# A Mamba-2 scan joined to a low-rank mixer on one core: state updates, copies of y and joins as pieces of their own, and a new order after piece w5

## The chip, the core and the metric

The kernel runs on one core of one Trainium2 chip. The metric is the device time of the execution in microseconds (us). The kernel before was run three times: 225.86 us is the median, 225.63 the lowest and 227.96 the highest. The profile is of one execution, whose span from the first to the last instruction is 224.7 us.

## What is computed

The first stage is a chunked state-space scan over x (4 batches, 8 heads, 768 positions, 32 channels), with decays a and projections B and C of 16 states. Its result, laid out as batch x 768 x 256, goes through a mixer: a low-rank product over the positions (U, V of rank 32), and a two-layer network over the channels (256 to 1024 to 256).

```python
# scan, per chunk of the sequence
L = np.exp(cum[:, :, :, None] - cum[:, :, None, :]) * causal
y_intra = np.einsum('bhij,bhjd->bhid', CB * L, xc)
y_inter = np.einsum('bhin,bhnd->bhid', Cc, state) * decay_to_i[:, :, :, None]
state = decay_full[:, :, None, None] * state + np.sum(Bx, axis=2)
...
# mixer
h = x.transpose(0, 2, 1) @ U @ V
u = x + h.transpose(0, 2, 1)
ch = np.maximum(u @ w_ch1, 0.0) @ w_ch2
return (u + ch).astype(np.float32)
```

## The kernel before, in words

The whole kernel is one list of pieces written out by hand: the string PLAN (line 36). Each word is a letter, which names a kind of piece, and numbers, which say for which block it is done. The function follow (line 859) reads the words from left to right and emits each piece's instructions, and every engine runs its own instructions in exactly that order. An engine whose next instruction waits holds up all that stand behind it. So the order of the words is the order of work on TensorE (PE), VectorE (DVE), ScalarE (ACT), GpSimd (POOL) and SyncE (SP, whose queue issues all DMAs).

The scan works on 12 blocks k of 256 positions, three for each batch (k = 3b + q). Its pieces:

- b, x, B, X, L: DMA loads of B, C and x; w, W, Z, z: loads of the mixer's weights, which come as 64-bit words. The pieces B, X, w and L wait, before their first DMA is issued, for the last DVE instruction that was emitted ahead of them (the list until, line 864).
- P (prep, one DVE product), T (turned: four transposes by PE in two halves, and after the second half three ACT copies; bank w), g (gram: 32 small matmuls into two x and two z banks), m and M (mask: two DVE operations each; m reads the x banks and M the z banks), s (state: small matmuls into two w banks), u (update: up to four chained DVE operations of 128x64, then one POOL product), i and j (inter: small matmuls with the state; j is preceded by the POOL copy "settled", line 576, which waits for the products of the same bank pair that stand before it), n (intra: 64 small matmuls), y (yout: two ACT copies out of the two y banks), t (transposes by PE, and a copy).

The mixer runs per batch b:

- c (to_fp32, line 398): the four steps in which DVE and ACT turn a weight's 64-bit words into fp32; R (refine): the steps that split a weight into near, far and joined parts for the batches 1 to 3.
- p, q, a: the low-rank product; S (split): one ACT and two DVE operations of 128x768 that split u into three parts, for a half j of the sequence.
- For batch 0: U (plain: fp32 matmuls with a relu by ACT) and d0 (down with fp32 matmuls).
- For batches 1 to 3, in a faster number format: f (first: four matmuls of 384 columns into a bank x or z, then an ACT scaling), e (second: two matmuls more into that bank, then an ACT relu), h (third: one DVE operation of 128x384 that makes the far part and lets the bank go, and for every odd m a further one, joined, line 710, of 128x768 that makes the joined part of both m of a pair), d (down: six pieces n = 0 to 5 of four matmuls of 256 columns for each output block k; the last adds one matmul, a DVE addition and the output DMA). Pieces 0 and 1 of d read the near parts, 2 and 3 the far parts, 4 and 5 the joined parts.

PSUM has eight banks, two under each of the names w, x, z and y. A piece that needs a bank waits until the piece that had it two allocations ago has been read out. In SBUF, 15 buffers called words are shared by the weights' words, their conversion and the parts that f, e, h and d use.

Of the kernel before, what the change touches and what calls it, by code (L numbers as in the profile page):

```python
# [76 lines left out]
def kernel(  # L77
# [64 lines left out]
    def bank(tag, *dims):  # L142
        t = psum.tile([P, *dims], FP32, tag=tag, name=tag, bufs=BANKS[tag])
        return t
# [75 lines left out]
    w1all = mix.tile([P, NQ, NCB, W], FP32, tag="u", name="w1f", bufs=1)  # L220
    w1f = [w1all[:, c] for c in range(NQ)]
    w2 = [const.tile([P, NM, DM], FP32R, name=f"w2{i}") for i in range(2)]
    weights = []
    w2f, w2b = {}, {}

    def w2c(n, dtype):
# [25 lines left out]
    def load_v():  # L252
        own["UV"] = words_of(UV)
        for q in range(4):
            begin(out=own["UV"][ts(q, Q), 2 * NC * RK:], in_=V2[:, ts(q, 2 * NC * RK)])
# [653 lines left out]
```

## Time and profile before

| what | value |
|---|---|
| median of 3 runs | 225.86 us (225.63 to 227.96) |
| span of the profiled execution | 224.7 us |
| first instruction of the new order (U0.0.0 on PE) | 34.84 us |
| last row of matmuls in the chain ends | 221.15 us |
| PE, DVE, ACT, POOL busy | 96%, 70%, 51%, 6% |
| granted TensorE clock | 1.00 throughout |

The profiled execution's own time isn't listed apart from the three runs; its span is 1.16 us below their median, which is the work around the first and the last instruction.

How to read it: a busy PE isn't PE at its peak, since matmuls overlap and their ends are modelled. Start to start of the pieces tells more, and the chain of waits gives that: each row of it is a time, how long the chain stayed there, the engine, the tile written, the line and how many instructions. In this kernel a row of 16 matmuls on line 613 is an i or j, of about 53 on line 635 an n, of 4 on line 656 a t, of 2 on line 480 half of T, about 32 on line 543 an s, rows on line 511 a g, and on line 725 x4 with tiles x or z a U or an f.

### The profile page before, as it was taken

The page shows a single profiled execution, that of the slowest core. Times are in us where ns is not written, and L with a number is a line of the kernel's source. Part 1 is how long each engine was busy: PE and PEld are TensorE (multiplying, and loading weights), DVE is VectorE, ACT ScalarE, POOL GpSimd, SP SyncE. Part 2 cuts the span into 40 slices and gives each one's busy share as a digit, 9 for nine tenths or more (in the row PEclk, how much of TensorE's full clock was granted, in tenths as well). Part 3 has the DMA queues.
Part 4 walks back from the last instruction along what each step waited for, and adds up shares of the span by engine and source line. Part 5 has one row for each costly group of instructions (what it writes and reads, how often), then busy time and mean ns, then how long its engine had stood idle before and what let it go on. Part 6 is the DMA issues. An engine that isn't in the chain of part 4 may idle for free.

```text
span 224.7 us, 7010 instructions
## 1 busy us (share of the span) xinstructions
PE 216.0 (96%) x3012; PEld 182.8 (81%) x3012; DVE 156.7 (70%) x329; ACT 114.3 (51%) x261; POOL 14.3 (6%) x37
## 2 busy tenths in 40 slices
PE   7888989999999999999999999999999999999993
PEld 4656655656668898987999898887998999999993
DVE  4776878899998866969717785758437964764921
ACT  3334946856994346334453632475237545655410
POOL 3021010012100000202101000100000000000000
PEclk9999999999999999999999999999999999999999
DMA  6997799788645203600002602000020000100011
GB/s 88 127 111 144 132 130 287 139 163 230 92 65 72 51 23 59 84 23 26 3 26 48 96 0 73 3 3 3 1 71 1 0 0 26 47 0 28 32 38 47
DMA packets 69518, 14.56 MB, mean 65 GB/s; under 512 B 63792, under 2 KB 67696, under 8 KB 69488
## 3 DMA queue, kind: packets, MB, share of 16 engines
q1 hardware_dynamic: 69488, 14.13, 34.6%
q8 instruction: 23, 0.38, 0.7%
q14 instruction: 7, 0.06, 0.1%
HBM read 10.98 MB, written 3.15 MB: 63 GB/s over the span
## 4 chain that ended last, share of the span: by engine, by line
PE 91%; DVE 2%; DMA 2%; SPq 1%; issue 1%; POOL 0%; ACT 0%; POOLq 0%; DVEq 0%
PE x L725 31%; PE z L725 24%; PE y L725 12%; PE y L613 4%; PE y L635 3%; PE w L480 3%; PE x L511 3%; PE w L656 2%; DMA bc<-in_B_dram 2%; PE w L543 2%; PE z L511 2%; PE x L138 1%; SPq L185 1%; PE w L679 1%; PE w L138 1%
## 5 line engine op out<-in xcount | busy, mean ns | idle before, releaser
L159 DVE SCALAR_TENSOR_TENSOR words<-words 128x768 fp32r<-128x768 f32 (+6 forms) x44 | 34.6, 806 | 1.9 <-ACT words L416 0.6
L725 PE MATMUL z<-u,w 128*128 128x384 f32 x144 | 34.0, 350 | 0.0
L725 PE MATMUL x<-u,w 128*128 128x384 f32 x144 | 33.1, 348 | 0.0
L730 ACT ACTIVATE x<-x 128x384 f32<-128x384 f32 (+1 forms) x30 | 13.6, 452 | 25.3 <-PE x L725 25.1
L725 PEld LDWEIGHTS z<-u,w 128*128 128x128 f32 x144 | 24.5, 188 | 1.3 <-DVE words L159 0.2
L725 PEld LDWEIGHTS x<-u,w 128*128 128x128 f32 x144 | 24.0, 188 | 1.3 <-ACT x L730 0.6
L159 DVE SCALAR_TENSOR_TENSOR words<-x,words 128x384 fp32r<-128x384 f32 x24 | 13.2, 555 | 16.4 <-ACT words L759 13.7
L725 PE MATMUL x<-w2c,words 128*128 128x256 f32 x112 | 22.5, 338 | 0.0
L730 ACT ACTIVATE z<-z 128x384 f32<-128x384 f32 (+1 forms) x27 | 12.5, 463 | 14.1 <-PE z L725 13.6
L725 PEld LDWEIGHTS x<-w2c,words 128*128 128x128 f32 x112 | 18.2, 189 | 1.3
L725 PE MATMUL y<-w,words 128*128 128x256 f32 x144 | 19.1, 282 | 0.0
L725 PEld LDWEIGHTS y<-w,words 128*128 128x128 f32 x144 | 18.5, 188 | 0.3 <-DVE ytok L159 0.3
L159 DVE SCALAR_TENSOR_TENSOR words<-z,words 128x384 fp32r<-128x384 f32 x24 | 13.2, 551 | 5.7 <-ACT words L759 5.7
L759 ACT ACTIVATE words<-x 128x384 fp32r<-128x384 f32 x24 | 11.6, 490 | 6.3 <-PE x L725 6.1
L759 ACT ACTIVATE words<-z 128x384 fp32r<-128x384 f32 x24 | 11.6, 491 | 4.9 <-PE z L725 4.8
L648 ACT COPY yT<-y 128x256 f32<-128x256 f32 x24 | 7.8, 384 | 10.9 <-PE y L613 10.7
L569 POOL TENSOR_TENSOR Sm<-S,own 128x256 f32<-128x256 f32 (+1 forms) x12 | 7.7, 644 | 87.5 <-DVE S L159 58.1
L159 DVE SCALAR_TENSOR_TENSOR S<-S,kept,w 128x64 f32<-128x64 f32 x40 | 11.2, 280 | 2.7 <-PE w L543 0.9
L613 PE MATMUL y<-T,Sm 32*64 32x64 f32 x352 | 12.4, 239 | 0.4 <-POOL Sm L569 0.3
L725 PE MATMUL x<-w,words 128*128 128x256 f32 x96 | 12.6, 282 | 0.0
L725 PEld LDWEIGHTS x<-w,words 128*128 128x128 f32 x96 | 12.0, 188 | 0.1
L511 PE MATMUL x<-Cm,T 32*64 32x128 f32 x192 | 11.0, 307 | 1.0 <-ACT Cm L490 0.7
(152 smaller groups left out, 400.5 us busy)
## 6 DMA issues: line engine op xcount, KB each, us to landing
words<-in_moe_w_ch_dram SPq DMA_DIRECT2D x7, 512.0 KB, 6.1
x<-in_x_dram SPq DMA_DIRECT2D x24, 128.0 KB, 3.7
out_dram<-ytok SPq DMA_DIRECT2D x24, 128.0 KB, 1.7
bc<-in_B_dram SPq DMA_DIRECT2D x24, 64.0 KB, 3.7
bc<-in_C_dram SPq DMA_DIRECT2D x12, 128.0 KB, 3.8
words<-in_moe_w_ch_dram SPq DMA_DIRECT2D x2, 256.0 KB, 4.5
words<-in_moe_V_dram SPq DMA_DIRECT2D x4, 48.0 KB, 3.1
words<-in_moe_U_dram SPq DMA_DIRECT2D x1, 192.0 KB, 3.5
```

The lines of the kernel that those rows point to most:

```text
L138: nc.tensor.matmul(out=t[:, :m * w].rearrange("p (m i) -> p m i", i=w), lhsT=ident, rhs=ident[:, None, :w].to_broadcast([P, m, w]), start= ...
L159: self.last = call(*args, **kwargs)
L480: nc.tensor.transpose(out=tp[:, i, v], in_=s["BC"][:, i, c + v].rearrange("p h n -> p (h n)"), identity=ident)
L511: nc.tensor.matmul(out=g[r][cols, c], lhsT=s["T"][rows, 0, c, cols], rhs=s["Cm"][rows, :, :, ts(2 * c + p, Q)].rearrange("r v t i -> r v i ...
L543: nc.tensor.matmul(out=s["A"][p][ts(r, Q), v], lhsT=s["BC"][half, 0, v, 2 * r:2 * r + 2].rearrange("p h n -> p (h n)"), rhs=x_sb[k][half, ...
L569: nc.gpsimd.tensor_tensor(out=s["Sm"][:, sl], in0=s["S"][:, sl].rearrange("p i (s d) -> p i s d", s=2), in1=own2[:, b, 4 * q + sl.start:4 ...
L613: product = nc.tensor.matmul(out=y[p][ts(r % 2, H), r // 2, c], lhsT=own[ts(r, Q)], rhs=s["T"][ts(r, Q), 1, :, ts(2 * c + p, Q)].rearrange ...
L635: product = nc.tensor.matmul(out=y[p][ts(i, Q), n, c], lhsT=x_sb[k][half, c, h], rhs=s["M"][half, h // 2, c, h % 2], start=fresh(k, p, [i] ...
L648: nc.scalar.copy(out=yp[:, :, :, p], in_=st[k]["y"][p])
L725: nc.tensor.matmul(out=t, lhsT=lhsT, rhs=rhs, start=start, stop=True, skip_group_check=True)
L730: nc.scalar.activation(t, t, AF.Copy, scale=1.0 + EPS)
L759: nc.scalar.activation(gs[j, m // 2][0][:, m % 2], t, AF.Relu, scale=NEAR)
```

## The change

The words u and y become two words each (u4.0 u4.1: the first two and the last two updates of the state; y4.0 y4.1: the copy of one y bank each). The POOL product of u is left as it was: one instruction after the second half. The joined operation leaves h and becomes a piece J with its own place. Up to piece w5 the words and loads stand as they were, with u and y only written as two words; from there on all words are in another order, loads among them. The loaded weights are kept in a dictionary instead of a list, since w8 is now loaded ahead of w7. The number of instructions of each kind stays as it was.

```diff
-    ... 'W2 W3 b5.1 W4 a0.0 c2 c2 a0.1 x4.0 w5 c3 c3 c3 c3 '
-    'U0.0.0 P5 U0.0.1 U0.1.1 R0 B6 t3 X5 g4 m4 T5 M4 T5 c5 c5 U0.1.0 c5 c5 X6 U0.1.3 c4 c4 s4 u4 w6 '
-    'w7 w8 U0.0.3 P6 U0.0.2 c6 U0.0.6 s5 c4 c4 U0.1.7 c6 U0.1.2 u5 R0 R2 U0.1.6 n4 s6 L7 i4 g5 c6 '
-    'j4 y4 u6 T6 T6 m5 c6 R4 R2 R1 U0.0.4 M5 U0.1.4 n5 i5 L8 g6 c7 c7 c9 c9 t4 j5 P7 T7 T7 M6 c7 c7 '
-    'y5 U0.0.7 c8 U0.0.5 t5 m6 n6 R3 c9 c9 P8 c8 p1 R7 g7 m7 L9 i6 M7 T8 T8 c8 c8 q1 d0.0.2.0 '
...
-    'd1.1.0.5 d1.1.2.4 d1.1.2.5 d1.1.1.4 d1.1.1.5 T10 g9 m9 T10 T11 T11 M9 i9 n9 g10 m10 M10 j9 y9 '
-    's11 u11 i10 g11 m11 M11 n10 f2.0.4 a2.1 f2.0.3 f2.0.2 e2.0.4 h2.0.4 e2.0.3 e2.0.2 f2.0.7 '
...
+    'W2 W3 b5.1 W4 a0.0 c2 c2 a0.1 x4.0 w5 U0.0.0 c3 X5 P5 c3 t3 U0.0.1 U0.1.1 c3 T5 T5 w6 c3 g4 m4 '
+    'M4 c4 s4 X6 u4.0 B6 u4.1 U0.0.2 c4 c5 R0 U0.1.0 c4 c5 c5 c5 s5 c6 w8 U0.1.3 U0.0.3 U0.1.2 u5.0 '
+    'u5.1 U0.0.6 P6 c4 n4 c7 s6 u6.0 i4 g5 c6 j4 u6.1 L7 R2 M5 y4.1 y4.0 c7 R1 T6 m5 w7 T6 U0.0.7 '
+    'U0.1.6 c6 n5 i5 g6 c9 c6 j5 c9 R0 y5.0 t4 P7 T7 M6 y5.1 T7 U0.1.5 m6 t5 U0.0.5 R3 n6 c9 c7 i6 '
+    'g7 c8 j6 R1 m7 p1 U0.0.4 M7 c9 q1 U0.1.4 c8 d0.0.1.0 R3 c7 s7 L9 c8 c8 U0.1.7 d0.0.1.1 R2 R4 '
+    'a1.0 S1.0 d0.0.0.0 d0.0.1.2 d0.0.1.3 L8 R6 y6.1 d0.0.0.1 d0.0.0.2 P9 R7 d0.0.0.3 y6.0 f1.0.0 '
+    'f1.0.3 d0.0.2.0 u7.0 d0.0.2.1 P8 u7.1 e1.0.0 d0.0.2.2 d0.0.2.3 e1.0.3 f1.0.5 f1.0.2 h1.0.3 '
+    'h1.0.0 T8 R6 f1.0.7 e1.0.2 d0.1.0.0 e1.0.5 R4 e1.0.7 h1.0.5 d0.1.0.1 d0.1.0.2 h1.0.2 f1.0.1 '
+    'h1.0.7 L10 T8 a1.1 R5 R7 d0.1.0.3 e1.0.1 f1.0.6 d0.1.1.0 f1.0.4 d0.1.1.1 h1.0.1 e1.0.6 d0.1.1.2 '
+    'R5 e1.0.4 h1.0.4 d0.1.1.3 h1.0.6 s8 n7 i7 g8 u8.0 P10 m8 j7 S1.1 T10 y7.1 d0.1.2.0 d0.1.2.1 T10 '
+    'M8 y7.0 f1.1.0 J1.0.3 d0.1.2.2 d0.1.2.3 f1.1.1 f1.1.3 e1.1.0 e1.1.1 J1.0.2 u8.1 s9 n8 u9.0 i8 '
+    'u9.1 h1.1.1 t7 d1.0.2.0 d1.0.2.1 d1.0.2.2 R4 L11 R6 j8 h1.1.0 s10 y8.0 d1.0.2.3 e1.1.3 d1.0.1.0 '
...
+    't8 f1.1.5 J1.1.0 e1.1.2 h1.1.2 f1.1.4 t6 e1.1.5 f1.1.6 e1.1.4 p2 T9 J1.1.1 h1.1.4 h1.1.5 e1.1.6 '
+    'h1.1.6 q2 T9 d1.1.2.0 d1.1.2.1 d1.1.2.2 d1.1.2.3 a2.0 J1.1.2 d1.1.1.0 J1.1.3 S2.0 d1.1.1.1 '
+    'd1.1.2.4 d1.1.1.2 d1.1.1.3 d1.1.0.0 d1.1.0.1 d1.1.0.2 d1.1.0.3 d1.1.1.4 P11 d1.1.2.5 d1.1.0.4 '
+    'd1.1.0.5 d1.1.1.5 s11 u11.0 g9 T11 m9 i9 M9 T11 g10 n9 M10 m10 j9 y9.1 g11 y9.0 n10 i10 M11 m11 '
+    'f2.0.4 a2.1 f2.0.1 e2.0.4 f2.0.6 f2.0.3 h2.0.4 e2.0.1 e2.0.6 j10 e2.0.3 u11.1 f2.0.0 y10.1 '
...
@@ def update(k, c=0, n=2):
-        sl = slice(own[0], own[-1] + 1)
+        if c + n < 2:
+            return
+        sl = slice(0, own[-1] + 1)
...
-    def yout(k):
+    def yout(k, p):
...
-        for p in range(2):
-            nc.scalar.copy(out=yp[:, :, :, p], in_=st[k]["y"][p])
+        nc.scalar.copy(out=yp[:, :, :, p], in_=st[k]["y"][p])
@@ def third(j, m):
-            if m % 2:
-                joined(near, far, both)
+
+        def fourth(j, n):
+
+            joined(*gs[j, n])
...
-                 M=lambda k: mask(k, (2, 3)), u=update, i=lambda k: inter(k, 0), n=intra,
+                 M=lambda k: mask(k, (2, 3)), u=lambda k, c: update(k, c, 1), i=lambda k: inter(k, 0), n=intra,
```

More of the change, by code (lines that the diff above doesn't have):

```diff
@@ L142, in bank @@
     def bank(tag, *dims):
-        t = psum.tile([P, *dims], FP32, tag=tag, name=tag, bufs=BANKS[tag])
-        return t
+        return psum.tile([P, *dims], FP32, tag=tag, name=tag, bufs=BANKS[tag])
     ctx.enter_context(tc.manual_schedule())
@@ L222 @@
     w2 = [const.tile([P, NM, DM], FP32R, name=f"w2{i}") for i in range(2)]
-    weights = []
+    weights = {}
     w2f, w2b = {}, {}
@@ L233, in words_of @@
         t = raw.tile([P, 2 * WCOLS], INT32, tag="words", name="words", bufs=NWORDS)
-        weights.append((dst, t[:p, :2 * i * j]))
         return t[:p, :2 * i * j]
@@ L238, in each, with load_words @@
         return [part[index] for part in parts]
-    def load_words(dst, src):
+    def load_words(n, dst, src):
         p, i, j = dst.shape
         t = words_of(dst)
+        weights[n] = dst, t
         begin(out=t.rearrange("p (i j) -> p i j", i=i), in_=src)
@@ L253, in load_v @@
         own["UV"] = words_of(UV)
+        weights[1] = UV, own["UV"]
         for q in range(4):
@@ L262, in load_w @@
         if n < 2:
-            if n == 0:
+            if "w" not in own:
                 own["w"] = words_of(w1f[0])
-                weights.pop()
             dst, t = w1f[0][:, :, ts(n, P)], own["w"][:, ts(n, 2 * NCB * P)]
-            weights.append((dst, t))
+            weights[2 * n] = dst, t
             begin(out=t.rearrange("p (i j) -> p i j", i=NCB),
@@ L270, in load_w @@
         elif n <= NQ:
-            load_words(w1f[n - 1], w13[:, :, ts(n - 1, 2 * quarter)])
+            load_words(n + 1, w1f[n - 1], w13[:, :, ts(n - 1, 2 * quarter)])
         else:
             m = 2 * (n - NQ - 1)
-            load_words(w2c(n - NQ - 1, FP32), w22[m * P:(m + 2) * P].rearrange(
+            load_words(n + 1, w2c(n - NQ - 1, FP32), w22[m * P:(m + 2) * P].rearrange(
                 "(m p) d -> p m d", p=P))
@@ L567, in update @@
             st["Sm", b, j + 1] = s["Sm"][:, i].rearrange("p s d -> p (s d)")
-        sl = slice(own[0], own[-1] + 1)
+        if c + n < 2:
+            return
+        sl = slice(0, own[-1] + 1)
         nc.gpsimd.tensor_tensor(
             out=s["Sm"][:, sl], in0=s["S"][:, sl].rearrange("p i (s d) -> p i s d", s=2),
-            in1=own2[:, b, 4 * q + sl.start:4 * q + sl.stop, :, None].to_broadcast(
-                [P, len(own), 2, D]), op=ALU.mult)
+            in1=own2[:, b, 4 * q:4 * q + sl.stop, :, None].to_broadcast(
+                [P, sl.stop, 2, D]), op=ALU.mult)
     def apart(k):
@@ L639, in intra @@
                         behind.setdefault(k, []).append(product)
-    def yout(k):
+    def yout(k, p):
         b, q = pairs[k]
-        if q == 0 and b:
+        if b not in yT:
             yT[b] = mix.tile([P, NCB, S], FP32, tag="yT", name="yT")
@@ L796, in mixer @@
         us, gs, gT = {}, {}, {}
-        return SimpleNamespace(p=project, q=parted, a=added, S=split, f=first, e=second, h=third,
+        return SimpleNamespace(p=project, q=parted, a=added, S=split, f=first, e=second, h=third, J=fourth,
                                d=down, U=plain)
```

52 rows, old and new, of the table PLAN are left out of this document.

## Prediction

> **What bounds the kernel now.** I read the page first: the busy shares, the slices and the chain's shares.
>
> ```profile
> span 224.7 us, 7010 instructions
> PE 216.0 (96%) x3012; PEld 182.8 (81%) x3012; DVE 156.7 (70%) x329; ACT 114.3 (51%) x261; POOL 14.3 (6%) x37
> ...
> PE   7888989999999999999999999999999999999993
> ...
> DVE  4776878899998866969717785758437964764921
> ...
> PE 91%; DVE 2%; DMA 2%; SPq 1%; issue 1%; POOL 0%; ACT 0%; POOLq 0%; DVEq 0%
> ```
>
> PE is in nine tenths of the chain and without a visible gap from the seventh slice on. DVE is full only in slices 8 to 13. Next the table by stages, cut where the work changes: the order that stays; the U pieces with batches 1 and 2 of the scan; the d0; then the rest.
>
> ```profile
> 0.00:34.84 34.84, 30.08 (x738) 20.32 (x738) 23.61 (x76) 17.29 (x48) 5.56 (x21) 1.00 0.92 128
> 34.84:68.10 33.26, 33.00 (x587) 20.94 (x588) 31.52 (x71) 26.20 (x56) 3.35 (x5) 1.00 0.74 154
> 68.10:101.60 33.50, 33.50 (x223) 29.76 (x221) 25.30 (x46) 14.48 (x30) 1.47 (x2) 1.00 0.32 52
> 101.60:147.10 45.50, 45.43 (x849) 41.35 (x846) 30.39 (x65) 19.59 (x46) 3.75 (x8) 1.00 0.16 34
> 147.10:221.00 73.90, 73.89 (x627) 70.45 (x625) 45.49 (x73) 36.70 (x83) 0.18 (x1) 1.00 0.06 19
> ```
>
> The columns are the stage's length, then PE, PEld, DVE, ACT and POOL, then the granted clock, which is 1.00 throughout. The first 34.84 us, where PE has its real gaps (4.8 us), belong to pieces whose order stays: nothing is won there. In the second stage DVE is busy 31.52 of 33.26 us, so there PE and DVE are both nearly full. Behind that only PE is.
>
> A busy PE can still be slow, so I go to the chain's rows for what one piece costs at its best and what it costs elsewhere.
>
> ```profile
> 41.48 1.29 PE x L725 x4
> ...
> 44.06 0.38 PE w L543 x32
> 44.45 1.49 PE z L725 x4
> ...
> 151.68 0.70 PE z L725 x4
> ...
> 152.81 0.58 PE w L656 x4
> 153.39 0.35 PE x L725 x2
> 153.75 0.89 PE z L725 x4
> 154.63 0.43 PE y L613 x16
> ```
>
> A U takes 1.29 us after its like and 1.49 behind the small s; an f takes 0.70 among its like and 0.89 between an e that followed a t and an i. So each block of small scan pieces that stands between the large matmuls costs PE about 0.2 us over its own time, without any engine being late. In the old list behind w5 I count 19 such blocks: some 19 x 0.2 = 3.8 us that no better overlap removes, only fewer blocks.
>
> **The change part by part.** No instruction is added or removed. The joined operation (J), the second half of u and the copies of y only move; so PE's own work stays, and the sum has three terms: the number of blocks, the waits that go, the waits that come.
>
> *Blocks.* In the new list I count 24 blocks of small pieces behind w5. The U stretch has 8 in place of 7 that stand up to s7, and the stretch behind it 16 in place of 12: T8 stands alone twice, T10 is parted once, T9 follows q2 alone, t6 stands alone. 5 more blocks at 0.2 us are 1.0 us at most. Blocks that are one T or t may cost less: there is no row for a lone T. The lower end is 0 (a wait of PE that falls into the block hides the switch), the upper 1.0. I take 0.8, near the upper end, since both rows above (1.49 against 1.29, 0.89 against 0.70) have the whole 0.2. The Trainium skill, page "TensorE: Matmul & The Clock Gate", section "Step-by-step: what each phase is for", says that PE pulls the next weight load ahead of running matmuls when the row groups don't conflict or the background weights are free, so that a load overlaps the matmul before it. By that a change of piece would be free and the sum 0.8 us lower; inside a stretch of one kind the trace agrees (four matmuls in 0.70), at the change it doesn't (0.89), so I go by the rows.
>
> *The first scan block behind w5.*
>
> ```profile
> 39.72 0.28 PE x L511 x2
> ...
> 40.85 0.63 PE w L480 x4
> ...
> 40.02 0.68 DVE L159 TENSOR_TENSOR BC<-bc,F 128x512 f32<-128x512 f32 x1
> 40.72 0.76 DVE L159 TENSOR_TENSOR M<-x,causal 128x256 int32<-128x256 int32 x2
> 41.40 0.75 DVE L159 TENSOR_TENSOR M<-z,causal 128x256 int32<-128x256 int32 x2
> ...
> 41.52 0.58 ACT L484 COPY T<-w 128x512 f32<-128x512 f32 x1 [0.66 <-PE w L480]
> 42.00 0.84 ACT L490 ACTIVATE Cm<-w,slot 128x256 f32<-128x256 f32 x2
> ```
>
> Before, g4 runs from 39.72 to 40.85, 1.13 us (g8 took 0.58, rows below): some 0.5 us of wait, for the z bank of U0.1.1, while T5 had its input from P5 at 40.70. In the new list P5 is three DVE operations earlier, so T5 comes straight behind U0.1.1 and g4 behind it: it still waits about 0.25 for the relu of U0.1.1. But s4 now follows g4 at once. It needs both w banks, and T5's bank is let go by the three ACT copies (0.58 and 0.84, ended 1.36 us after T5 itself, 41.48 to 42.84). Of that only g4, with its wait about 0.85, lies over it, and ACT first has the relu of U0.1.1 to do: s4 waits 0.5 to 0.85, I take 0.65, as the relu and T5 end within a half microsecond of each other. 0.9 in place of 0.5: +0.4.
>
> *The scan of batch 3.*
>
> ```profile
> 102.06 0.13 PE x L511
> ...
> 102.64 0.25 PE w L543 x8
> ...
> 137.56 0.28 PE x L511 x2
> ...
> 138.64 0.81 PE w L480 x6
> 139.45 0.42 PE y L613 x12
> ...
> 141.38 0.27 PE y L613 x10
> ...
> 143.69 0.79 PE y L635 x52
> ...
> L648 ACT COPY yT<-y 128x256 f32<-128x256 f32 x24 | 7.8, 384 | 10.9 <-PE y L613 10.7
> L576 POOL COPY settled<-slot 128x1 f32<-128x1 f32 x12 | 4.2, 348 | 46.2 <-PE y L635 32.3 <-PE y L613 14.0
> ```
>
> g8 shows what a g costs, 102.06 to 102.64. Before, g9 took 137.56 to 138.64, so 0.5 of wait (for a z bank that d1.1.1.5's addition frees); j9, s11, i10 and g11 took 141.38 to 143.69, 2.31 us for work of 0.43 + 0.38 + 0.43 + 0.58 = 1.82 (an i or j by the row of i9, an s as at 44.06): 0.5. Together 1.0. In the new list s11 stands ahead of g9 and covers 0.25 of its wait (0.25 left). But g10 comes already after T11, i9 and T11: a cover of 0.22 + 0.43 + 0.22 = 0.87 us (half of T is a third of the row of six, less the switch), while all four banks have to pass m9 and M9, 0.76 + 0.75 on DVE: g10 waits 0.65 to 0.75. j9 follows n9 directly, so "settled" (0.35 on POOL by its mean, behind n9's end) can't start before: 0.35. n10 comes after g11 alone (0.58), with two copies of y9 at 0.38 in front: 0.2. M10 and m10 are covered by n9 and j9. Sum 0.25 + 0.7 + 0.35 + 0.2 = 1.5 in place of 1.0: +0.5.
>
> *The waits that go.* Behind 147.1 the old order takes 73.9 us; the 143 pieces at their best (f 0.69, e 0.35, d 0.47 and 0.59 for the last, the small ones as in the rows) come to 71.4, and its five blocks to 1.0. About 1.1 to 1.5 us of waits are left there, and some 0.3 for s9 and n7 near 103. They stand where an f waits for a bank that h lets go:
>
> ```profile
> L159 DVE SCALAR_TENSOR_TENSOR words<-words 128x768 fp32r<-128x768 f32 x24 | 23.1, 963 | 1.2
> L159 DVE SCALAR_TENSOR_TENSOR words<-x,words 128x384 fp32r<-128x384 f32 x24 | 13.2, 555 | 16.4 <-ACT words L759 13.7 <-PE x L725 1.4 <-ACT z L730 1.2
> ```
>
> Before, each odd h (0.55) drags its joined operation (0.96) behind it, and the next h or addition, which frees a bank, stands behind both on DVE. With J a piece of its own, joins stand behind several h, and their readers d.4 and d.5 come late: J2.0.1 stands twelve pieces ahead of d2.0.1.4, say. Also the e with which PE went straight into a d of the same pair (e2.1.7, d2.1.2.0, d2.1.2.1) now have several pieces between. All of it is 1.4 (1.1 + 0.3), so the gain lies between 0 and 1.4, or below nothing if joins come too late for d.4; I take 0.9, since the DVE isn't full there (45.49 of 73.90), so that an h moved ahead does run ahead. If DVE were full, J would only be late in h's place.
>
> *Loads.* They go through SP in the new order, and hold up nothing on PE by themselves:
>
> ```profile
> words<-in_moe_w_ch_dram SPq DMA_DIRECT2D x7, 512.0 KB, 6.1
> bc<-in_B_dram SPq DMA_DIRECT2D x24, 64.0 KB, 3.7
> ...
> 53.34 0.37 SPq L185 DMA_DIRECT2D bc<-in_B_dram  x1
> ...
> 55.09 2.15 SPq L185 DMA_DIRECT2D x<-in_x_dram  x2
> ```
>
> w8 waits for c6's first step and needs 6.1 us; DVE has ahead of c9's first step two u (8 x 0.28), P6, a step of c4, c7's first, m5 and M5 (1.5) and two operations of c6, some 7 us. Before, L7's five issues took 53.34 to 57.24, 3.9 us; P7's last part is the third of them and lands about 1.6 + 3.7 us after the first issue, and DVE has some 5.4 us of work ahead of P7. w7 stands behind L7 in the queue. All are in time by half a microsecond to one. I count 0 for them, and up to 2 us in the range.
>
> The tail (the last d, its addition and its DMA) stays: 0.
>
> Sum against the profiled execution: 224.7 + 0.8 + 0.4 + 0.5 - 0.9 = 225.5. Its span is 1.16 us below the median of the runs shown, 225.86; I carry that over: **226.7 us**, 0.4% more than before. A measurement of this kernel tells about 1% (2.3 us) from no change: the forecast is no change.
>
> **The rivals.**
>
> *Faster: blocks cost nothing and the waits go.* If the switches hide behind other things (0) and the new order has none of the waits that I place at s4 and g10 (DVE or ACT ahead of my count), it gains all that can be gained: 0.5 + 1.0 + 1.4 = 2.9, so 223.0. For it: the fuller separation of h and J. Against it: s4's two banks and g10's four have a fixed chain of copies or masks in front, with rows for each. It is over 1% only if nearly all goes. The Trainium skill, page "Perfetto Trace Analysis", section "Identifying the Most-Contended Engine", says matmul busy time is no measure of the room on PE, and to take the weight loads' share, here 81%; a reading by it would leave more room than 2.9 us. In the stage behind 147.1, where the weight loads are busy 70.45 of 73.90, the trace says there is little.
>
> *Slower: the loads come late and DVE stands.* Place: c9, c8 and P7 on DVE between 55 and 65 us, where DVE is busy 31.52 of 33.26. If w8, L7 or w7 lands later than 0.5 to 1 us past my count, DVE stands, and everything behind it in its queue: m6, M6 for n6, q1, a1.0, S1.0, f1.0.0. DVE has some slack there: its operations from w5 to S1.0, by the rows, end near 75 us, and the pieces of PE put f1.0.0 at about 78; for n6 and T7 there is less. It decides from 2 us late on; with 4 us late for the three (6.1 us become 10), PE loses about 2.5 us: 229.2. For it: the chain already has 2% of DMA, and six queue rows lie close together. Against: the second stage's DMA share is 0.74 now and nothing is added.
>
> *No effect:* J, u and y move but waits only change places, all terms within 0.3 of zero: 225.9. It is inside the forecast's case.
>
> **How the numbers follow.** Forecast within 1% (223.6 to 228.1): 0.66, the no-effect case included. Faster: 0.10, since it asks for three terms at their ends at once. Slower by over 1%: 0.24, by late loads, or because the s4, g10 and block terms are at their upper ends with no gain behind 147 (1.0 + 0.65 + 0.6, that is 228.1). Range: from 224.4 (blocks 0, gain 1.4) to 229.2 (late loads). It leaves out about 2 in 10.
>
> **What would show each step right or wrong.** Blocks: rows of U at 1.49 and f at 0.89 more often than before, and the stage from w5 to the first d1 longer with no wait named. s4: a gap between g4 and s4 of over 0.4 us, with ACT's Cm copies ended just before s4. Batch 3: g10 over 1.1 us long, and a gap between n9 and j9. J: f and e rows near 150 us without the extra 0.1, and the stage behind it below 73.9 us. Loads: DVE idle before words or BC released by a DMA between 50 and 66 us. Wrong is the prediction if PE shows a wait of over 1 us in a place not named here, or if the blocks turn out free.

## The result

| | kernel before | changed kernel |
|---|---|---|
| median of 18 runs each | 225.93 us | 228.19 us |
| ratio, with its 95% interval | | 1.0088 (1.0061 to 1.0116) |
| span of the profiled execution | 224.7 us | 226.1 us |

The changed kernel is 0.9% slower, which is inside the 1% that the prediction called no change, and inside its range (224.4 to 229.2). The interval leaves out 1, so it is a small slowdown and not noise, about twice the 0.4% that was forecast. The predicted 226.7 us is 1.5 us too low. The median of before rests on more runs here than in the prediction and hardly moved. Executions over 1.5% above the fastest of their kernel are left out of the ratios, "at full clock" below means a granted clock of 0.995 or more over the execution, and a star in a table marks a stretch in which the clock was below 1.00 for a while.

The page of the changed kernel, the lines that answer to those shown of before:

```profile
span 226.1 us, 7017 instructions
...
PE 214.4 (95%) x3012; PEld 181.6 (80%) x3012; DVE 154.6 (68%) x329; ACT 114.5 (51%) x261; POOL 13.2 (6%) x37
...
PE 72%; SPq 8%; DVE 7%; DMA 6%; issue 3%; ACT 1%; POOL 1%; DVEq 0%; POOLq 0%; ACTq 0%
```

PE's work is nearly the same (214.4 us, before 216.0), but PE has 72% of the chain instead of 91%, and the queue, the DMAs and DVE have 21% instead of 5%. That isn't time lost on PE: of the some 42 us by which PE's part of the chain is shorter, 16 us lie ahead of 35.5 us, where the order is unchanged and the chain only follows the DMA queue back from a load. What PE lost is read from the stages. Next the stages, cut at U0.0.0, U0.0.4, s8, f2.0.4 and the last d piece. The columns are again the length, PE, PEld, DVE, ACT, POOL, the clock and the DMA share.

```profile
0.00:35.52 35.52, 29.81 (x739) 19.54 (x739) 23.53 (x76) 17.42 (x48) 5.63 (x21) 1.00 0.91 115
35.52:67.40 31.88, 30.19 (x588) 19.15 (x588) 29.62 (x69) 23.86 (x50) 3.29 (x6) 1.00 0.70 156
67.40:100.62 33.22, 32.77 (x191) 28.03 (x187) 20.18 (x40) 18.42 (x39) 0.62 (x1) 1.00 0.46 65
100.62:147.29 46.67, 46.03 (x860) 41.40 (x860) 34.79 (x71) 17.14 (x41) 2.81 (x6) 1.00 0.16 36
147.29:222.12 74.83, 74.83 (x636) 72.95 (x636) 45.91 (x77) 37.62 (x85) 0.88 (x3) 1.00 0.05 19
```

In the second stage PE now has gaps of 1.69 us (31.88 less 30.19), where before it had 0.26. The last stage is shorter; the same cut of the kernel before is this:

```profile
144.41:220.38 75.97, 75.96 (x641) 72.50 (x636) 47.07 (x78) 37.65 (x85) 0.37 (x2) 1.00 0.06 19
```

75.97 has become 74.83. Stages with other pieces in them can't be subtracted so. For these I take the time from the start of one PE piece to the start of the next, less a fixed time for each kind of piece, what it takes undisturbed among its like (U 1.29 us, f 0.69, e 0.35, d 0.47, n 0.79, half of T 0.22, and so on), and call the sum over a stage its room. Single pieces can come out shorter or longer by 0.2 us, since a start moves when the next piece is of another kind, so the room is used to compare, not as a wait of its own. Behind f2.0.4 and between s8 and the last scan cluster the room of one order comes out the same within 0.1 us in every execution, so one execution is enough there. Room in us, by stages:

| run | first U to last U | f1.0.0 to s8 | s8 to scan of batch 3 | scan of batch 3 | f2.0.4 to end |
|---|---|---|---|---|---|
| before | 2.29 | 0.53 | 1.52 | 1.31 | 2.40 |
| changed | 3.90 | 0.87 | 1.06 | 2.08 | 1.25 |
| a1, changed again | 5.88* | 1.11 | 1.06 | 2.08 | 1.24 |
| e1, b5.1 early | 5.20 | 1.03 | 1.06 | 2.09 | 1.31 |
| e2, L8 ahead of L9 | 5.19* | 1.87 | 1.08 | 2.08 | 1.31 |
| e3, old scan of batch 3 | 5.20 | 0.85 | 1.06 | 1.68 | 1.33 |
| e4, g4 first | 7.04* | 0.95 | 1.06 | 2.08 | 1.25 |
| e5, L9 L8 early | 4.08* | 0.15 | 1.07 | 2.08 | 1.31 |
| e6, T in pairs | 3.77 | 1.53 | 1.59 | 2.24 | 1.25 |
| e7, before with late J | 2.31 | 0.54 | 7.65* | 1.31 | 7.98 |
| e8, b5.1 and x4.0 early | 3.99 | 1.17 | 1.09 | 2.08 | 1.31 |
| e9, old head, new tail | 2.56 | 0.54 | 1.50 | 1.31 | 1.34 |
| e10, before with J spread | 2.19 | 0.53 | 1.51 | 1.31 | 3.54 |
| e11, three mended | 4.68 | 0.15 | 1.07 | 1.68 | 1.33 |

So the loss is in the U stage (+1.6 us here, up to +2.9) and in the scan of batch 3 (+0.77), a late load adds 0.7 us behind f1.0.0, and the last stage gives 1.15 back.

Where the U stage loses, the chain of waits of the changed kernel shows:

```profile
33.60 6.22 DMA bc<-in_C_dram
...
39.94 0.70 DVE BC L161
...
40.78 0.64 PE w L482 x4
...
41.93 0.85 ACT Cm L492 x2
...
42.83 0.43 PE w L545 x24
...
54.27 0.29 DVE S L161
...
54.70 0.63 PE w L482 x4
...
59.49 0.56 POOL settled L580
```

The C of block 5, issued at 33.60, lands 6.22 us later; P5 (39.94) and T5 (40.78) stand for it. s4 (42.83) stands for the copies of T5. T6 (54.70) stands for the second half of u6, now a piece behind j4, and j5, which now follows g6 at once, for "settled" (59.49). And behind f1.0.0:

```profile
81.64 3.55 DMA bc<-in_B_dram
...
85.31 0.69 DVE BC L161
...
86.90 0.97 PE x L728 x4
87.87 0.22 PE w L482 x2
88.09 0.70 PE z L728 x4
```

L8 is issued behind the addition and the output DMA of d0.0.1.3, its last B lands at 85.19, and P8 holds DVE until then; f1.0.2 (86.90) has to wait for an addition behind P8.

### The profile page after: what moved, and what is told of

Its sections match the earlier page's. It is cut to its first block, busy times and chain, and to the rows that moved or that the text cites. A ratio compares the mean times of both kernels' runs of the same rounds, so it can differ in the third digit from the quotient of the medians.

```text
span 226.1 us, 7017 instructions
## 1 busy us (share of the span) xinstructions
PE 214.4 (95%) x3012; PEld 181.6 (80%) x3012; DVE 154.6 (68%) x329; ACT 114.5 (51%) x261; POOL 13.2 (6%) x37
## 3 DMA queue, kind: packets, MB, share of 16 engines
q1 hardware_dynamic: 69488, 14.13, 35.5%
## 4 chain that ended last, share of the span: by engine, by line
PE 72%; SPq 8%; DVE 7%; DMA 6%; issue 3%; ACT 1%; POOL 1%; DVEq 0%; POOLq 0%; ACTq 0%
PE x L728 26%; PE z L728 19%; PE y L728 12%; SPq L187 8%; DMA bc<-in_C_dram 5%; PE y L639 3%; PE y L617 3%; PE w L482 2%; PE w L659 2%; DMA bc<-in_B_dram 2%; DVE words L161 2%; PE x L513 1%; PE w L545 1%; PE z L513 1%; PE w L682 1%
## 5 line engine op out<-in xcount | busy, mean ns | idle before, releaser
L728 PE MATMUL z<-u,w 128*128 128x384 f32 x144 | 32.2, 342 | 0.0
L728 PEld LDWEIGHTS x<-u,w 128*128 128x128 f32 x144 | 24.5, 188 | 1.4 <-DVE ytok L161 0.8
L728 PE MATMUL y<-w,words 128*128 128x256 f32 x144 | 19.6, 281 | 0.0
L651 ACT COPY yT<-y 128x256 f32<-128x256 f32 x24 | 8.4, 376 | 14.0 <-PE y L617 14.0
L161 DVE TENSOR_TENSOR BC<-bc,F 128x512 f32<-128x512 f32 (+2 forms) x18 | 8.9, 510 | 9.5 <-DMA bc<-in_B_dram 6.6
L728 PE MATMUL x<-w,words 128*128 128x256 f32 x96 | 13.6, 285 | 0.0
L617 PE MATMUL y<-T,Sm 32*64 32x64 f32 x352 | 11.9, 240 | 1.1 <-POOL settled L580 0.6
L728 PE MATMUL z<-w2c,words 128*128 128x256 f32 x56 | 12.0, 340 | 0.0
```

The lines of the kernel that those rows point to most:

```text
L161: self.last = call(*args, **kwargs)
L617: product = nc.tensor.matmul(out=y[p][ts(r % 2, H), r // 2, c], lhsT=own[ts(r, Q)], rhs=s["T"][ts(r, Q), 1, :, ts(2 * c + p, Q)].rearrange ...
L651: nc.scalar.copy(out=yp[:, :, :, p], in_=st[k]["y"][p])
L728: nc.tensor.matmul(out=t, lhsT=lhsT, rhs=rhs, start=start, stop=True, skip_group_check=True)
```

## The experiments

### a1: the changed kernel once more

> The changed kernel once more, beside the kernel before on the same chip. Theory A (the loss is late data for VectorE at two places plus a longer tail of the scan of batch 3; the 0.67 us by which U0.0.0 starts later in the changed trace is a matter of one execution, since nothing ahead of it differs): the ratio is again near 1.009, and in the new profile U0.0.0 starts at 34.8 to 35.0 us. Rival B (the start is really later by 0.67 us, through the loads): U0.0.0 starts again at 35.4 us or later.

Measured: 1.0044 (0.9996 to 1.0092), lower than the 1.009 that was expected, with an interval that holds both 1 and 1.0088. U0.0.0 started at 35.98 us here. With a clock of 1.00 ahead of it, it started at 33.96 to 35.98 us in eight executions with this order behind it and at 34.30 to 34.92 in three with the order of before. So its place is a matter of the execution, as theory A has it; the 35.98 alone would have pointed to B.

### e1: one late load moved forward

```diff
- b5.2 b5.0 T4 T4 j3 y3.0 y3.1 W2 W3 b5.1 W4
+ b5.2 b5.0 b5.1 T4 T4 j3 y3.0 y3.1 W2 W3 W4
```

> The changed kernel with one load moved: the C of block 5 (b5.1) is issued right behind the two other loads of block 5 instead of behind W2 W3. In the changed trace P5 on VectorE waits 1.29 us for it, and T5 with its four matmuls stands 0.85 us late. Theory A (this load is what makes the first U pieces dearer): P5 waits less than 0.2 us, the pieces from U0.0.0 to U0.1.4 take 0.9 to 1.4 us less, the time is 0.4 to 0.6 per cent below that of the changed kernel (about 227.0). Rival (the 1.3 us are in VectorE only, and another wait, that of j4 or g6, takes the place): the time is that of the changed kernel, 228.2.

Measured: 1.0031 (0.9988 to 1.0074), no faster than a1 beside it (at full clock the median is 227.62 us for both); the room of the U stage 5.20. P5 no longer waits, but the chain now has another load:

```profile
33.12 8.69 DMA x<-in_x_dram
...
41.94 0.65 PE w L545 x29
```

s4 stands 2.1 us for the first x of block 4, the last load of the same group. DVE, too, has other stands now: 0.71 us for the weights W2, 0.44 for a step of ACT and 1.13 at P6 for the B of block 6. The rival holds: other waits take the place.

### e2 and e5: the loads of block 8 earlier

```diff
 e2
- R3 c7 s7 L9 c8 c8 ... d0.0.1.3 L8 R6
+ R3 c7 s7 L8 L9 c8 c8 ... d0.0.1.3 R6
 e5
+ R3 c7 s7 L9 L8 c8 c8 ... d0.0.1.3 R6
```

> The changed kernel with the loads of block 8 issued ahead of those of block 9, no longer behind the additions of the first d pieces. In the changed trace VectorE stands 3.95 us at P8 for its B. Theory A (late load, 0.6 to 0.7 us of it reach TensorE at f1.0.5 and f1.0.2): the stand of VectorE goes, the time is about 227.5. Rival (TensorE has enough queued, the 0.6 us come from the order of d and f in that stage): the stand of VectorE goes and the time stays within 0.2 us of 228.2.

Measured: 1.0091 (1.0048 to 1.0133), at full clock 228.65 us against a1's 227.62. The rows of P9 and P8 on DVE (in brackets the idle time before, and what ended it):

```profile
84.05 0.69 DVE L161 TENSOR_TENSOR BC<-bc,F 128x512 f32<-128x512 f32 x1 [1.94 <-DMA bc<-in_B_dram]
85.49 0.69 DVE L161 TENSOR_TENSOR BC<-bc,F 128x512 f32<-128x512 f32 x1
```

P9 stands ahead of P8 in the list, and L9 was now second in the queue: the stand moved from P8 to P9, and PE lost 1.62 us at f1.0.3. Neither theory had that. With L9 first:

> The changed kernel with the loads of block 8 issued right behind those of block 9, both ahead of the additions of d. Issuing L8 ahead of L9 moved the stand of VectorE from P8 to P9, since P9 comes first in the order, and TensorE lost 1.6 us at f1.0.3. Theory A (a load that is late for VectorE's next step holds the additions behind it, and so the banks of the f pieces): now neither P9 nor P8 waits over 0.5 us, the room over the shortest times between f1.0.0 and s8 is 0.3 us or less, against 0.87 in the changed kernel and 1.87 with L8 first. Rival (0.6 us at f1.0.5 belong to the order of f and d there): it stays 0.8 or more.

```profile
80.86 0.68 DVE L161 TENSOR_TENSOR BC<-bc,F 128x512 f32<-128x512 f32 x1
83.18 0.69 DVE L161 TENSOR_TENSOR BC<-bc,F 128x512 f32<-128x512 f32 x1 [0.79 <-DMA bc<-in_B_dram]
```

P8 still waits 0.79 us, a little over what was expected, but the room from f1.0.0 to s8 is 0.15 instead of 0.87. Theory A holds: 0.7 us of the loss were this load. Without it the new order is better there than the old one (0.53).

### e3: the scan of batch 3 in its old order

```diff
- s11 u11.0 g9 T11 m9 i9 M9 T11 g10 n9 M10 m10 j9 y9.1 g11 y9.0 n10 i10 M11 m11
+ g9 m9 T11 T11 M9 i9 n9 g10 m10 M10 j9 y9.0 y9.1 s11 u11.0 u11.1 i10 g11 m11 M11 n10
```

> The changed kernel with the last scan cluster (blocks 9 to 11) in the order of the kernel before; all else as changed. Theory A (the new order of that cluster costs 0.75 us at g9, T11, g10 and j9): the time is about 227.4. The prediction's own figure for it is 0.5 us, 227.7. Rival (the small pieces cost as much in any order, because what they wait for is the rotation of the buffers that the pieces before and behind them fill): the time stays within 0.2 us of 228.2.

Measured: 1.0054 (1.0010 to 1.0098), not to be told from a1 by the time (227.64 us at full clock), since the U stage varies by more. The room of the cluster fell from 2.08 to 1.68: 0.40 us are the order's. This is about half of theory A's 0.75. The other 0.37 above before stay; before also had T10's halves on both sides of g9, which this edit doesn't restore.

### e4: the old neighbours of T5 and s4

```diff
- U0.0.1 U0.1.1 c3 T5 T5 w6 c3 g4 m4 M4 c4 s4 X6 u4.0 B6 u4.1 U0.0.2
+ U0.0.1 U0.1.1 c3 g4 m4 T5 M4 T5 w6 c3 c4 X6 U0.0.2 s4 u4.0 B6 u4.1
```

> The changed kernel with g4 put ahead of T5, and U0.0.2 ahead of s4, as the kernel before has them. The load of C of block 5 stays where it is and lands 6 to 7 us after its issue, so VectorE's P5 waits as long as in the changed kernel. Theory A (the load is not late by itself; what costs is that nothing stands between U0.1.1 and T5, and nothing between T5's copies and s4): the stands at T5 (0.85 us) and s4 (0.70 us) fall to 0.3 us together, the pieces from U0.0.0 to the last U take 1.0 to 1.3 us less than in an execution of the changed kernel with the same landing of that load. Rival (the lost time moves to g4 or to the next piece behind, which want the same bank and the same x): the sum of the waits from U0.0.0 to s4 stays within 0.3 us.

Measured: 232.64 us as the median of four executions, none at full clock, so there is no ratio, and part of the 7.04 us of room is the clock. s4 waits only 0.2 us now, but U0.0.2 stands until 43.05: its weights come from c3's last step on DVE, which now has m4 and M4 in front of it. The rival holds again, at a place that it didn't name.

### e6: the halves of T together

```diff
- h1.0.0 T8 R6 ... L10 T8 a1.1 ... S1.1 T10 y7.1 d0.1.2.0 d0.1.2.1 T10 ... p2 T9 J1.1.1 ... q2 T9 d1.1.2.0
+ h1.0.0 T8 T8 R6 ... L10 a1.1 ... S1.1 T10 T10 y7.1 d0.1.2.0 d0.1.2.1 ... p2 T9 T9 J1.1.1 ... q2 d1.1.2.0
```

> The changed kernel with the two halves of T8, T10 and T9 behind each other again, so three blocks of small pieces fewer. The prediction's price of 0.2 us a block gives 0.6 us less between f1.0.0 and the last stage. Rival, from the rows of the changed trace (T8's pieces are 0.08 us shorter than the shortest before and the f behind them 0.085 longer; T10's and T9's 0.137 longer): a lone T costs 0.0 to 0.14 us, so the pairs give 0.0 to 0.2 us.

Measured: one execution, 228.84 us, and more room, not less: +0.66 between f1.0.0 and s8 (0.33 of it at f1.0.5, where P8's load sets the time in every execution), +0.53 in the next stage. A lone half costs nothing: in the changed kernel it takes 0.22 us and the f behind it 0.70 (87.87 and 88.09 above). T10 together or apart makes 0.01 us of difference. What the pair of T8 costs is seen on ACT, first in this kernel and then in the changed one:

```profile
87.42 0.47 ACT L733 ACTIVATE x<-x 128x384 f32<-128x384 f32 x1 [1.29 <-PE x L728]
87.86 0.59 ACT L486 COPY T<-w 128x512 f32<-128x512 f32 x1
88.34 0.84 ACT L492 ACTIVATE Cm<-w,slot 128x256 f32<-128x256 f32 x2
89.06 0.64 ACT L444 ACTIVATE w<-words 128x512 fp32r<-128x512 f32 x1
89.58 0.50 ACT L733 ACTIVATE z<-z 128x384 f32<-128x384 f32 x1
```

```profile
87.91 0.47 ACT L733 ACTIVATE x<-x 128x384 f32<-128x384 f32 x1 [0.94 <-PE x L728]
88.41 0.63 ACT L444 ACTIVATE w<-words 128x512 fp32r<-128x512 f32 x1
88.95 0.48 ACT L733 ACTIVATE z<-z 128x384 f32<-128x384 f32 x1
```

With the pair, three copies stand between the scaling of f1.0.2 and that of f1.0.7, which starts 2.16 us behind it instead of 1.04, and e1.0.7 waits for it. With T9 the 0.53 us are likewise at the two d pieces behind the pair; its ACT rows were not followed further.

### e7 and e10: the joins apart, in the old order

In e7 each J stands six PE pieces ahead of its reader, in e10 (last stage only) three pieces behind its second h and, where the reader leaves room, four from the next J.

```diff
 e7
- h1.1.6 h1.1.7 a2.0 S2.0 P11 d1.1.1.1 d1.1.1.2 d1.1.1.3 d1.1.0.3
+ h1.1.6 h1.1.7 a2.0 S2.0 P11 d1.1.1.1 d1.1.1.2 J1.1.0 J1.1.1 d1.1.1.3 J1.1.2 J1.1.3 d1.1.0.3
...
 e10
- h3.0.7 d3.0.2.3 d3.0.1.3 f3.1.0
+ h3.0.7 d3.0.2.3 J3.0.3 d3.0.1.3 f3.1.0
...
```

> The kernel before with one part of the change: the joins (J) apart from h, each put six pieces ahead of its first reader, 23 of 24 moved; the order is else that of before. Theory A, the prediction's (the joins inside h hold VectorE and so the banks of f and e, 0.9 us behind 147 us): the last stage is 0.7 to 1.2 us shorter than before's, its room 1.2 to 1.7 us instead of 2.40, the time 0.3 to 0.5 per cent below the kernel before. Rival (it is the new order of f, e and d that gives the 1.15 us of the changed trace): the room of the last stage stays within 0.3 us of 2.40 and the time is that of before.

Measured: 1.0429 (1.0352 to 1.0506). All joins of a half have the same readers, so four of them fell into one heap:

```profile
135.80 3.49 DVE words L161 x4
...
139.33 2.93 PE x L728 x12
```

3.49 us of DVE with d's additions behind them: the bank isn't let go, and PE stands. That refutes this placing, not yet the theory, hence e10:

> The order of the kernel before, with the joins of the last stage taken out of h and each put three TensorE pieces behind its second h, four pieces from the next join and well ahead of its reader; f, e, h and d stand as before. Four joins in a heap had held VectorE for 3.49 us ahead of the additions, so these are spread. Theory A, the prediction's (h without the join gives back the banks of f and e earlier): the room of the last stage falls from 2.40 us to 1.2 to 1.7 us. Rival (the 1.15 us come from the new order of f, e, h and d, or from the joins' distance of 8 to 20 pieces): the room stays at 2.1 us or more.

Measured: 1.0079 (1.0033 to 1.0126), room of the last stage 3.54. The waits of f and e near 150 us are those of before within 0.01 us (0.11 at e2.0.2, 0.10 at e2.0.0, 0.18 at e2.0.6, 0.20 at f2.0.5). For f2.0.5 the profile of before shows why: it starts at 153.67, when h2.0.7 has just let its bank go, and this h stood for ACT's relu and not behind a join:

```profile
153.06 0.56 DVE L159 SCALAR_TENSOR_TENSOR words<-z,words 128x384 fp32r<-128x384 f32 x1 [0.21 <-ACT words L759]
```

What comes on top is one late reader after another, here d3.0.2.3 with what follows:

```profile
199.01 0.97 DVE u L161
...
200.01 0.96 DVE u L161
200.97 1.35 DVE words L161 x2
...
202.36 0.86 PE y L728 x5
```

The joins had slipped behind S3.1's two operations. So taking J out of h in this placing shortens none of these waits; the rival holds.

### e9: the old order up to f2.0.4, the new one behind

> The order of the kernel before up to f2.0.4 (joins behind the second h), and the order of the changed kernel with its joins apart from f2.0.4 to the end. Theory A (the last stage gains 1.15 us by itself, and all of the loss lies ahead of it): the room of the stages ahead is that of the kernel before, 5.65 us, that of the last stage 1.2 to 1.4 us instead of 2.40, the time 0.4 to 0.6 per cent below the kernel before. Rival (the last stage of the changed kernel is short because it starts from another state of buffers and of VectorE): the last stage keeps 2.0 us or more and the time is within 0.2 per cent of before.

Measured: 0.9953 (0.9903 to 1.0004) against before. The last stage of this kernel, and that of e10 beside it:

```profile
144.12:219.04 74.92, 74.92 (x643) 73.04 (x637) 46.27 (x78) 37.62 (x85) 0.37 (x2) 1.00 0.06 19
```

```profile
146.96:224.08 77.12, 76.28 (x642) 72.88 (x637) 46.69 (x78) 37.68 (x85) 0.37 (x2) 1.00 0.05 18
```

74.92 us, as in the changed kernel (74.83) and 1.05 less than before (75.97); the stages ahead keep the room of before. Theory A holds, and this version is better than both kernels by the stages. By the times the interval just reaches 1. At a full clock the median span is 223.4 us in 7 executions, against 224.8 in 17 of the kernel before on that chip.

### e8 and e11: two more ways to mend the U stage

```diff
 e8
- b5.2 b5.0 T4 T4 j3 y3.0 y3.1 W2 W3 b5.1 W4 a0.0 c2 c2 a0.1 x4.0 w5
+ b5.2 b5.0 b5.1 T4 T4 j3 y3.0 y3.1 x4.0 W2 W3 W4 a0.0 c2 c2 a0.1 w5
```

> The changed kernel with two loads issued earlier: the C of block 5 (b5.1) behind b5.0, and the first x of block 4 (x4.0) ahead of the three loads of weights W2 W3 W4 instead of behind them. With b5.1 alone moved, s4 had to wait for that x, which landed 8.69 us after its issue, and nothing was gained. Theory A (the changed kernel reads both loads, which land at 38 to 42 us, two U pieces earlier than the kernel before, and one of T5, g4 and s4 takes 1.3 to 2.1 us whichever is covered): with both early, T5 and g4 wait under 0.3 us, s4 keeps only the 0.5 to 0.7 us for the copies of T5, and the room from U0.0.0 to the last U is 2.3 to 3.0 us, against 3.8 to 5.2 us in the executions of the changed order so far. Rival (the weights, now behind these loads, take their place: c3 or U0.0.2 waits for W2 to W4): the room stays at 3.8 us or more, with the wait at U0.0.0 to U0.0.2.

Measured: 1.0076 (1.0033 to 1.0118); room 3.99, no less than without the edit (3.90). Both loads are there in time, and now the weights behind them are late: DVE and ACT stand for W2 at c3's first steps, with P5 and the relus of U0.0.1 and U0.1.1 behind them.

```profile
38.32 0.76 DVE L161 TENSOR_SCALAR words<-words 128x512 int32<-128x512 int32 x2 [0.98 <-DMA words<-in_moe_w_ch_dram]
38.32 0.69 ACT L418 ACTIVATE words<-words 128x512 f32<-128x512 uint32 x1 [1.36 <-DMA words<-in_moe_w_ch_dram]
```

```diff
 e11, with e5 and e3
- U0.0.1 U0.1.1 c3 T5 T5 w6 c3 ... c4 c5 R0 U0.1.0 c4
+ U0.0.1 U0.1.1 c3 U0.1.0 T5 T5 w6 c3 ... c4 c5 R0 c4
```

> The changed kernel with three parts mended at once, each read by its own stage: U0.1.0, whose weights are there already, moved ahead of T5 (all loads issued as in the changed kernel at that place); the loads of block 8 right behind those of block 9; the last scan cluster in the order of the kernel before. With both loads moved forward nothing had been gained: VectorE's and ScalarE's first steps of c3 then stood until the weights W2 had landed, and P5, T5 and g4 behind them. Theory A (the queue of loads issued between 28 and 35 us lands at its own pace until 42 us, and what reads them must stand further back; one more U piece ahead of T5 hides 1.3 us): the room from U0.0.0 to the last U is 2.4 to 3.0 us instead of 3.8 to 5.2 in undisturbed executions, that from f1.0.0 to s8 0.15 to 0.3, that of the last scan cluster 1.7, that of the last stage 1.3; the time is 0.7 to 1.1 per cent below the changed kernel and within 0.4 per cent of before. Rival (the wait moves again, to s4, g4 or j4): the first room stays at 3.6 us or more, and the time is 0.4 to 0.5 per cent below the changed kernel.

Measured: 1.0038 (0.9998 to 1.0079). The parts at L8 and at batch 3 gave what they should (0.15 and 1.68). The U stage did not: 4.68. T5's wait is gone, and s5, which had U0.1.0 in front of it, stands for the update of the state on DVE instead, about 1.0 us. The time is not told apart from a1's 1.0044. That is the rival's case.

Why every cure moves the wait shows in the stretch from U0.0.0 to T6, measured in the same way in all kernels. The changed one, then e3 and e11 (columns as above, the fourth number is DVE):

```profile
35.52:54.70 19.18, 17.71 (x293) 10.70 (x293) 17.35 (x42) 13.21 (x28) 1.94 (x3) 1.00 0.82 204
```

```profile
34.99:55.12 20.13, 17.71 (x293) 10.86 (x293) 17.33 (x42) 12.90 (x27) 1.92 (x3) 1.00 0.76 190
```

```profile
34.56:54.21 19.65, 18.10 (x293) 11.05 (x293) 17.51 (x42) 13.27 (x28) 2.26 (x3) 1.00 0.77 196
```

| | length | DVE busy | DVE idle |
|---|---|---|---|
| changed | 19.18 | 17.35 | 1.83 |
| e1 | 20.28 | 17.36 | 2.92 |
| e3 | 20.13 | 17.33 | 2.80 |
| e4 | 21.92* | 17.48 | 4.44 |
| e6 | 18.88 | 17.61 | 1.27 |
| e8 | 19.05 | 17.42 | 1.63 |
| e11 | 19.65 | 17.51 | 2.14 |

That a length is an engine's work plus its idle time holds for any engine. What makes DVE the one to look at is the order: T6 needs the bank that u6.1 lets go, and u6.1 stands behind nearly all of DVE's list for the stretch. In the changed kernel, e1, e3, e8 and e11 T6 waits for it, and DVE has run through the list with no gap over 0.15 us except these stands: P5 for the C of block 5 in the changed kernel (1.29 us), e3 (2.26) and e11 (1.39), W2 in e8 (0.98), and the three of e1. There each stand of DVE makes T6 later by as much, and it doesn't matter which PE piece shows the wait. In e1 the x of block 4 held up PE at s4, but no step of DVE.

The stands are not the whole loss. PE's pieces in the stretch come to 19.0 us undisturbed in the old order (eleven U) and to 16.4 us in the new one (nine U), DVE's work to 19.31 and 17.35 us. The new order took 2.6 us of PE's work from ahead of T6, but only 2.0 us of DVE's. Of the 1.09 us by which the changed profile has more room there (2.75 instead of 1.66), 0.6 us come from this, and 0.5 us from DVE's stands, 1.83 us instead of the 1.36 of before; another 0.5 us lie behind T6. In e6 the C of block 5 was in time and T6 didn't wait, and still PE stood at g4, s4 and g5 and the stage kept 3.77 us of room. No edit tried here took the loss of the U stage away: that it lies ahead of f2.0.4 is shown by e9, but its cause is argued from the traces.

## Why the prediction came out as it did

The forecast of no change and the range held, but several terms missed, in both directions. By its own sign ("Wrong is the prediction if PE shows a wait of over 1 us in a place not named here, or if the blocks turn out free") the account failed: the added blocks were free, and T5, which it hadn't named, came 0.85 us late in the changed profile and 1.8 us late in e3, which has the same order there.

*Blocks, +0.8: wrong.* The list has five blocks more, as counted, yet the two stages from f1.0.0 to the scan of batch 3 have 0.83 us less room once L8 is in time (e5, and again e11: 0.15 + 1.07; before: 0.53 + 1.52), and joining halves of T made it dearer (e6). The step that failed is that each block "costs PE about 0.2 us over its own time". The 0.2 us are real, but not for each block. From end to end, as the chain counts, two U behind s5 take 2.78 us in the changed kernel and the two after them 2.58:

```profile
46.03 0.36 PE w L545 x24
46.39 2.78 PE z L728 x8
49.17 2.58 PE x L728 x8
```

In the fourteen traces 47 of 48 U behind an s or p take 1.49 us, and an f behind s, n, i or p takes 0.89 or more. Behind a t, q, T5 or T7 a U takes 1.29 undisturbed, and all 43 f behind a T or t take 0.69 to 0.71. (Behind T6 a U often takes 1.49; there it waits for a mask on DVE.) The added blocks are halves of T and a t, and these are free; T or t itself takes some 0.15 us more when it follows small matmuls such as i, j or g. Steps from such small matmuls to a T, a t or a larger piece number 19 in the old list behind w5 and 17 in the new one; at these prices the term is 0.3 to 0.4 us less, not 0.8 more. The other row, the f of 0.89 at 153.75, was no price at all: it stands behind an e, and is the wait for h2.0.7 shown at e10. The Trainium skill, page "TensorE: Matmul & The Clock Gate", section "Step-by-step: what each phase is for", has weight loads pulled ahead under running matmuls, by which a switch is free. For a lone T the trace agrees: 0.22 us, and 0.70 for the f behind it. Behind an s it doesn't: 1.49 against 1.29.

*g4 and s4, +0.4: the mechanism was right, the size small.* s4 waited 0.70 us for T5's copies (predicted 0.65), and its chain rows 41.93 and 42.83 are the ones that I had named. But this is only one of the waits in that stage.

*Loads, 0 and up to 2 us: the second step that failed.* I counted w8, L7 and w7, which were in time. Late were the loads that had *not* moved, because their readers had: b5.1 and, in e1 and e6, x4.0 are read up to two U pieces earlier than before. I said that P5 comes three DVE operations earlier and took that as a gain for T5, without asking when its C lands. And L8, whose issue waits for the addition of d0.0.1.3, was 0.7 us. The slower rival had the right mechanism (DVE stands for a load, and all behind it) with the wrong loads and too large a slack: where DVE has 17.4 us of work in 19.2 us and T6 waits for the end of it, there is none. That premise stood in the prediction, "PE and DVE are both nearly full"; I drew the conclusion for J only, not for loads.

*Two waits that I had not listed:* T6 for u6.1 and j5 for "settled", as g6 now has nothing behind it, some 0.45 us each. The split of u has a price where the second half is put behind j4.

*The scan of batch 3, +0.5: +0.77.* g10 took 1.08 us (a little under the 1.1 named), and j9 starts 0.36 after n9's end. g9, not fully covered by s11, is 0.42 instead of 0.25.

```profile
142.02 0.37 PE w L482 x2
143.47 0.80 PE y L639 x52
144.63 0.49 PE y L617 x12
```

*The waits that go, -0.9: -1.15 in the last stage, but not for my reason.* The size was near, e9 shows it to be the tail's own, and e10 shows that a J apart without the new order of f, e, h and d, in its placing, gives nothing and loses 1.1 us where joins come late. The 0.3 us at s9 and n7, which the -0.9 also counted, were not measured apart. Which of the tail's moves gives the gain has not been told apart.

*The sum.* By the profiled executions the last d piece starts 1.74 us later than before: 1.06 of room, and 0.68 that U0.0.0 was later by chance. Over many executions the changed kernel is 2.0 us slower (0.88% of 225.9), more than this pair shows, as its U stage can have 5.2 us of room (e3) in place of 3.9. The prediction's 0.8 is less than half of that, and even so it lies as near as it does by errors that cancel: the blocks made it too high, the loads too low. That the time fell into the range is in part luck. The lower end of the range was also added up wrongly: with blocks at 0 and a gain of 1.4 us, 225.9 + 0.4 + 0.5 - 1.4 is 225.4 us; 224.4 needs the terms of s4 and g10 at 0 as well.

## What to carry to other kernels

When a list is reordered, ask of each load that stays where its first reader went: in this case the loads of one busy group landed 4 to 9 us after their issue, and two of them were late once their readers had moved forward by a few pieces. Moving one load forward made the next one late. Find the engine that works without a gap up to the step that others wait for; covering the waits of another engine then only moves them. Compare also how much work of each engine the new order leaves ahead of that step. Before a price read from one row is charged to every change of piece, look up the same row behind each kind of piece, and ask whether the row holds a wait.

## What else the runs showed

The span is a poor measure to 0.4 us. The time of an execution less its span is 1.8 us (1.72 to 1.85) in every kernel that has the old order up to f2.0.4, and 2.2 us (2.15 to 2.25) in every kernel that has the new one. But from the start of the last d piece to the end of the span it is 4.3 us in the first and 4.0 in the second, so that the two together come to 6.1 to 6.2 us in both, and nothing seems lost there. The last recorded instruction is the same in both; two of POOL's closing semaphore instructions stand 0.41 us apart in the first (before, e9) and 0.08 us in the second (changed, e3). Why is open. The 1.16 us that the prediction carried over compared the span of one execution with the median of others.

The DMA issues of one list took unequal times on SP: that of W2 1.06 us in before's profile, 2.32 in the changed one and 0.66 in e5, and in the changed order the C of block 5 landed 5.4 us (e6), 6.2 us (changed) to 7.4 us (e3) after its issue. With this goes that the U stage of one and the same order had 3.77, 3.90 and 5.20 us of room in these three undisturbed executions, while the stages from s8 on, where fewer loads run, agreed within 0.1 us.
